# Weight groups prepared one cell later, and a halo requested ahead of the first weights

## The chip, the cores and the metric

The kernel runs on one core of a Trainium2 chip. A core has five engines that each work through their own list of instructions in order: PE multiplies matrices, DVE and POOL work on vectors, ACT copies, casts and evaluates functions, and SP here only issues transfers, which 16 DMA engines carry out. The metric is device time in microseconds (us) of one execution; lower is better.

## The reference

A causal convolution over time with weights that differ per token and head, and after it two feed-forward layers. Shapes: x is (2, 4096, 192), there are 8 heads of 24 channels and 7 taps, and the layers go from 192 to 2048 and back to 192, for all 8192 tokens.

```python
# convolution: softmax over the 7 taps, then a weighted sum of 7 tokens
w = weight_gen - np.max(weight_gen, axis=-1, keepdims=True)
w = np.exp(w)
w = w / (np.sum(w, axis=-1, keepdims=True) + 1e-09)
x_pad = np.concatenate([np.zeros((B, 6, D)), x], axis=1)
x_unf = x_pad[:, np.arange(S)[:, None] + np.arange(K)[None, :], :].reshape(B, S, K, H, group)
x = np.einsum('bshk,bskhg->bshg', w, x_unf).reshape(B * S, D)
# first layer
h = x @ moe_w_in
g = np.where(h > 0.0, h, np.exp(np.minimum(h, 0.0)) - 1.0)
x = g @ moe_w_out
# second layer
h = x @ moe2_w_in
g = h * np.clip(h + 3.0, 0.0, 6.0) / 6.0
out = g @ moe2_w_out
```

x and weight_gen are float32. The layers' weight matrices are float64 in memory, which is why the kernel reads them as pairs of 32-bit words.

## The kernel before, in words

**Tiling.** The 128 partitions each own 64 tokens in a row. The tokens are taken in 16 *blocks* of 4 tokens per partition (512 tokens). Each layer's 2048 hidden columns are taken in 8 *slices* of 256. A *cell* is one layer, one block, one slice: 2 x 16 x 8 = 256 cells, first all of the first layer, then all of the second (`cells`, lines 494 and 495). Cell n is number n in that list, and cells 0 to 7 are block 0 of the first layer.

**Precision.** Products are made of two parts: x is split into xh and xl, a weight into a high part (`wi_h`, in `wo` the first columns) and a low part (`wi_l`), and three of the four cross products are summed. A cell has 18 matmuls for the first product (x by w_in into the two PSUM tiles `h`), and from cell 3 on the second product of the cell three before (g by w_out into `acca` and `accb`; `LAG` is 3).

**What a cell does outside PE.** ACT evaluates the activation from `h` (line 468 and 469, twice each, one per half), DVE ends it (line 485, `gate`), ACT rounds the result to the high part gh (line 475, `round_g`), DVE makes the low part gl (line 479, `rest_g`). A cell's `h` tiles are used again two cells on, so the gate has to be done by then.

**Weights.** They don't come ready: the 64-bit words have to be turned into a high and a low part on the core. A *unit* is one slice of w_in (kind i) or w_out (kind o). `groups` (line 544) puts the first layer's units together: group 0 is the first slice of w_in, groups 1 to 7 are two units each, group 8 is one. A unit of the first layer takes one step on ACT (`begin`, line 146), five on DVE (lines 150, 153, 157, 165, 174; at 157 ACT also casts the high part, line 167), then three matmuls on PE (`p5`, lines 179 to 181: their sum is the low part), and ACT's casts of that sum (`p6`, line 186). In groups 1 to 3 the intermediate words lie in the PSUM bank that `p5` writes next, so that `p5` has to wait for the last DVE step; from group 4 on they lie in SBUF.

**What orders it.** All of it is written out by hand in the loop at line 604; nothing is reordered after that. In cell n come: the matmuls of cell n; `p5` of group n+1; `round_g` of cell n-1 (while n is 1 to 7); activation and gate of both halves, with `p6` of group n+1 after them; then `wst.run(n)`, which issues the ACT and DVE steps of later groups; then `rest_g`. How many steps `run` issues follows from a table of tasks: each has a cell from which it may begin, a *due* cell and a count of steps, and enough steps are issued to have each task done before its due cell. For a unit group n of the first layer the due cell stands in line 545. When a group begins, the transfers of the next group's raw words are requested (`want`).

**Before cell 0** (lines 582 to 602) two things are made side by side: the convolution of block 0, half of it on DVE and half on POOL, and group 0. DVE's list takes their steps in turns. `load_block` (line 204) requests a block's tap weights `wt`, its own tokens in `xt`, and for blocks 0 and 1 the *halo*, the tokens before the block that another partition owns, by two transfers of 63 rows (line 218). For block 0 `between` is the request of group 0's raw words: three transfers. SP issues these requests one after the other in the order of the list.

Of the kernel before, what the change touches and what calls it, by code (L numbers as in the profile page):

```python
# [17 lines left out]
def kernel(  # L18
# [185 lines left out]
    def load_block(i, between=None):  # L204
        t0 = TM * i
        xt = xw.tile([P, TM + HALO, D], F32, tag="xt", name="xt", bufs=2)
        wt = xw.tile([P, TM * H, K], F32, tag="wt", name="wt", bufs=2)
        later(
            0, wt.rearrange("p a k -> p (a k)"), wv[:, t0:t0 + TM, :].rearrange("p t c -> p (t c)"))
        m = max(0, HALO - t0)  # L210
        later(0, xt[:, m:HALO + TM, :], xv[:, t0 - HALO + m:t0 + TM, :])
        if between:
            between()
        if m:

            for b in range(B):
                nc.gpsimd.memset(xt[b * PB:b * PB + 1, 0:m, :], 0.0)
                nc.sync.dma_start(
                    xt[b * PB + 1:(b + 1) * PB, 0:m, :],
                    xv[b * PB:(b + 1) * PB - 1, TP + t0 - HALO:TP + t0 - HALO + m, :])  # L220
        return xt, wt

    def attention(i):
# [283 lines left out]
    def later(n, out, in_):  # L507

        if now is None or now >= len(cells) or now < 2 and n == 0:
            nc.sync.dma_start(out, in_)  # L510
        else:
            waiting.append((now + n, out, in_))
# [29 lines left out]

    units = [(k, 0, q - (k == "o")) for q in range(NQ + 1) for k in "io" if 0 <= q - (k == "o") < NQ]
    groups = [units[:1]] + [units[n:n + 2] for n in range(1, len(units), 2)]
    wtasks = [[0, n - 2, len(g)] for n, g in enumerate(groups)]
    for n in range(2 * NQ):
        c = NQ * (n + 2) if n < NB - 2 else start2 + (NQ if n % 2 else 0)
        groups.append([("io"[n % 2], 1, n // 2)])
# [9 lines left out]
    def w_steps(n):  # L558
        def step(k, u):
            def s():  # L560
                if k < 0:
                    if u == 0:
                        want(n)
                        want(n + 1)
                        if groups[n][0][1] == 0:

                            fts[n] = act.tile([P, XN], F32, tag="z", name="f", bufs=2)
                    made[n][u].begin()
                else:
                    getattr(made[n][u], f"s{k}")()  # L570
            return s
        return [step(k, u) for k in range(-1, WS if groups[n][0][1] else 5) for u in range(len(groups[n]))]

    wtasks = [
        [b, d, ((WS if groups[n][0][1] else 5) + 1) * c, (lambda n: lambda: w_steps(n))(n)] for n, (b, d, c) in enumerate(wtasks) if n > 1]
# [5 lines left out]
    with tc.manual_schedule():  # L581
        nc.vector.memset(three, 3.0)
        nc.scalar.activation(warm, three, AF.Exp)
        blk[0] = load_block(0, lambda: want(0))
        make_identity(nc, ident)
        nc.scalar.copy(plus, ident)
        nc.scalar.mul(minus, ident, -1.0)
        blk[1] = load_block(1)

        todo = {"w": w_steps(0), "a": attention(0)}  # L590
# [13 lines left out]
        for n in range(len(cells) + LAG + 3):  # L604
# [54 lines left out]
            if n in loads:  # L659
                blk[loads[n]] = load_block(loads[n])  # L660
# [30 lines left out]
```

## Time and profile before

| | before |
|---|---|
| runs outside the profiler | 1232.46, 1232.89, 1233.21 us; median 1232.89 |
| span of the profiled execution | 1230.4 us |
| PE busy | 1193.3 us (97%) |
| weight loads of PE | 1053.3 us (86%) |
| DVE busy | 933.1 us (76%) |
| ACT busy | 855.9 us (70%) |
| POOL busy | 418.7 us (34%) |
| moved by DMA | 75.81 MB |

The span runs from the first to the last instruction. What lies between it and a run's time (2.49 us to the median) is start and end outside the instructions; the profile gives no other time of its own. PE is busy for all but 37 us. Where an engine sat idle ahead of an instruction, the trace names what released it.

### The profile page before, as it was taken

How to read it: one execution, taken by the hardware profiler on the slowest of the kernel's cores; microseconds unless marked ns; L12 is line 12 of the kernel's file. 1: busy time of each engine (PE TensorE's matmuls, PEld its weight loads, DVE VectorE, ACT ScalarE, POOL GpSimd, SP SyncE). 2: the span in 40 equal slices, each digit the busy share in tenths (PEclk: the TensorE clock that was granted, in tenths of full speed). 3: DMA queues.
4: the chain of work that ended last, by engine and by line, in shares of the span. 5: the costliest groups of instructions: out<-in, count | busy, mean ns of one | idle time of the engine just before them, and what ended most of it. 6: DMA issues, size and time to landing. Idle time of an engine off the chain costs nothing.

```text
span 1230.4 us, 25449 instructions
## 1 busy us (share of the span) xinstructions
PE 1193.3 (97%) x10176; PEld 1053.3 (86%) x10176; DVE 933.1 (76%) x1224; ACT 855.9 (70%) x1340; POOL 418.7 (34%) x234
## 2 busy tenths in 40 slices
PE   3799999999999999999999999999999999999998
PEld 2568898989999888999888888888888888888886
DVE  6778999999999999998677666666666666666663
ACT  2677888888888888888876665555666665666653
POOL 7438778877777877776000000000000000000000
PEclk9899999999999999999999999999999999999999
DMA  6432023222122222111211101111110111111110
GB/s 175 125 114 65 25 88 88 88 88 69 41 69 87 89 88 77 67 39 47 65 53 52 41 31 48 52 52 40 52 38 29 52 52 52 40 52 33 34 40 26
DMA packets 33430, 75.81 MB, mean 62 GB/s; under 512 B 4388, under 2 KB 16802, under 8 KB 33312
## 3 DMA queue, kind: packets, MB, share of 16 engines
q1 hardware_dynamic: 33312, 74.19, 20.8%
q8 instruction: 80, 1.31, 0.5%
q14 instruction: 38, 0.31, 0.1%
HBM read 36.43 MB, written 12.58 MB: 40 GB/s over the span
## 4 chain that ended last, share of the span: by engine, by line
PE 92%; DVE 3%; ACT 3%; DMA 1%; issue 1%; SPq 0%; DVEq 0%
PE h L448 43%; PE acca L448 29%; PE accb L448 19%; DVE gl L479 1%; ACT gh L475 1%; DMA xt<-in_x_dram 1%; DVE r L485 0%; ACT r L468 0%; ACT r L469 0%; PE acca L316 0%; DVE f L157 0%; PE acca L372 0%; PE acca L179 0%; PE aux L179 0%; DMA xl<-xl 0%
## 5 line engine op out<-in xcount | busy, mean ns | idle before, releaser
L448 PE MATMUL h<-xh,wi_l 64*128 64x512 f32 x1536 | 577.7, 397 | 4.8 <-ACT wi_l L186 4.8
L448 PE MATMUL h<-xh,wi_h 64*128 64x512 f32 x1536 | 572.7, 396 | 3.2 <-DVE xl L328 2.6
L448 PE MATMUL h<-xl,wi_h 64*128 64x512 f32 x1536 | 570.2, 395 | 0.8 <-DMA xl<-xl 0.8
L448 PE MATMUL acca<-gh,wo 64*128 64x512 f32 x2048 | 561.9, 393 | 0.3
L479 DVE TENSOR_TENSOR gl<-r,gh 128x1024 fp32r<-128x1024 f32 x256 | 394.6, 1541 | 63.3 <-ACT gh L475 62.1
L448 PEld LDWEIGHTS acca<-gh,wo 64*128 64x128 f32 x2048 | 378.0, 185 | 27.3 <-SPq L452 2.4
L471 ACT ACTIVATE r<-h,three 128x512 f32<-128x512 f32 x256 | 176.2, 688 | 222.7 <-PE h L448 114.9
L448 PE MATMUL accb<-gh,wo 64*128 64x512 f32 x1024 | 324.7, 396 | 0.0
L448 PE MATMUL accb<-gl,wo 64*128 64x512 f32 x1024 | 321.3, 393 | 0.3 <-DVE gl L479 0.3
L448 PE MATMUL acca<-gl,wo 64*128 64x512 f32 x1024 | 321.2, 393 | 0.0
L448 PEld LDWEIGHTS h<-xh,wi_l 64*128 64x128 f32 x1536 | 284.9, 186 | 24.6 <-ACT wi_l L186 6.0
L448 PEld LDWEIGHTS h<-xh,wi_h 64*128 64x128 f32 x1536 | 284.9, 186 | 23.0 <-DVE xl L328 2.8
L448 PEld LDWEIGHTS h<-xl,wi_h 64*128 64x128 f32 x1536 | 284.3, 186 | 20.1 <-DMA xl<-xl 1.4
L488 DVE SCALAR_TENSOR_TENSOR r<-r,h 128x512 f32<-128x512 f32 x256 | 175.9, 687 | 161.2 <-ACT r L471 160.4
L475 ACT CAST gh<-r 128x1024 fp32r<-128x1024 f32 x256 | 266.3, 1040 | 11.2 <-DVE r L485 10.5
L485 DVE SCALAR_TENSOR_TENSOR r<-r,h 128x512 f32<-128x512 f32 x256 | 173.2, 677 | 40.3 <-ACT r L469 39.5
L448 PEld LDWEIGHTS acca<-gl,wo 64*128 64x128 f32 x1024 | 189.4, 185 | 12.5
L448 PEld LDWEIGHTS accb<-gl,wo 64*128 64x128 f32 x1024 | 189.0, 185 | 12.7 <-DVE gl L479 0.7
L448 PEld LDWEIGHTS accb<-gh,wo 64*128 64x128 f32 x1024 | 186.6, 185 | 12.0 <-issue 1.4
L274 POOL TENSOR_TENSOR tmp<-xt,wt 128x768 f32<-128x768 f32 (+1 forms) x96 | 192.6, 2006 | 6.3
L468 ACT ACTIVATE r<-h 128x512 f32<-128x512 f32 x256 | 152.5, 596 | 51.8 <-PE acca L448 30.3
L469 ACT ACTIVATE r<-r 128x512 f32<-128x512 f32 x256 | 162.0, 633 | 8.1
(119 smaller groups left out, 731.1 us busy)
## 6 DMA issues: line engine op xcount, KB each, us to landing
xt<-in_x_dram SPq DMA_DIRECT2D x14, 960.0 KB, 5.5
xh<-xh SPq DMA_DIRECT2D x64, 192.0 KB, 2.7
xl<-xl SPq DMA_DIRECT2D x64, 192.0 KB, 2.8
raw<-in_moe_w_out_dram SPq DMA_DIRECT2D x16, 384.0 KB, 3.2
z<-z SPq DMA_DIRECT2D x16, 384.0 KB, 2.3
zin<-z SPq DMA_DIRECT2D x16, 384.0 KB, 3.0
out_dram<-ot SPq DMA_DIRECT2D x16, 384.0 KB, 4.0
raw<-in_moe_w_in_dram SPq DMA_DIRECT2D x16, 192.0 KB, 3.3
```

What stands on the lines that cost most here:

```text
L274: eng.tensor_tensor(o.rearrange("p t (h g) -> p t h g", g=G), xk, wk.rearrange("p (t h) g -> p t h g", h=H), op=ALU.mult)
L448: mm = nc.tensor.matmul(o, w, r, start=st, stop=sp).ins
L468: nc.scalar.activation(r, h, AF.Relu, scale=-1.0)
L469: nc.scalar.activation(r, r, AF.Exp, scale=-1.0)
L471: nc.scalar.activation(r, h, AF.Relu, bias=three)
L475: nc.scalar.copy(gg[n][0], rs[n])
L479: nc.vector.tensor_tensor(gl, rs.pop(n), gh.bitcast(F32), op=ALU.subtract)
L485: nc.vector.scalar_tensor_tensor(r, r, -1.0, h, op0=ALU.add, op1=ALU.max)
L488: nc.vector.scalar_tensor_tensor(r, r, 6.0, h, op0=ALU.min, op1=ALU.mult)
```

## The change

Two edits. In `load_block` the callback `between` is called behind the halo's requests where there is a halo, and ahead as before where there is none; only block 0 passes one. In the table of tasks the due cell of weight group n of the first layer goes from n-2 to n-1.

```diff
@@ load_block
         later(0, xt[:, m:HALO + TM, :], xv[:, t0 - HALO + m:t0 + TM, :])
-        if between:
+        if between and not m:
             between()
         if m:
 
             for b in range(B):
                 nc.gpsimd.memset(xt[b * PB:b * PB + 1, 0:m, :], 0.0)
                 nc.sync.dma_start(
                     xt[b * PB + 1:(b + 1) * PB, 0:m, :],
                     xv[b * PB:(b + 1) * PB - 1, TP + t0 - HALO:TP + t0 - HALO + m, :])
+            if between:
+                between()
         return xt, wt
@@ tasks of the weight groups
-    wtasks = [[0, n - 2, len(g)] for n, g in enumerate(groups)]
+    wtasks = [[0, n - 1, len(g)] for n, g in enumerate(groups)]
```

The first edit shows on SP, at the start of the program. `wt` and `xt` are block 0's tap weights and tokens, `63x1152` its halo, `raw` the words of weight group 0, and the last row is block 1's tap weights. Before:

```order
L510 DMA wt<-in_weight_gen_dram 128x224
L510 DMA xt<-in_x_dram 128x768
L510 DMA raw<-in_moe_w_in_dram 64x3x256
L510 DMA raw<-in_moe_w_in_dram 64x2x256
L510 DMA raw<-in_moe_w_in_dram 64x256
L218 DMA xt<-in_x_dram 63x1152 x2
L510 DMA wt<-in_weight_gen_dram 128x224
```

With the change:

```order
L512 DMA wt<-in_weight_gen_dram 128x224
L512 DMA xt<-in_x_dram 128x768
L218 DMA xt<-in_x_dram 63x1152 x2
L512 DMA raw<-in_moe_w_in_dram 64x3x256
L512 DMA raw<-in_moe_w_in_dram 64x2x256
L512 DMA raw<-in_moe_w_in_dram 64x256
L512 DMA wt<-in_weight_gen_dram 128x224
```

The two halo requests have moved past the three of the weights; DVE's, ACT's and POOL's lists at this place are as before, with group 0's steps at the same places between those of the convolution.

The second edit shows on ACT between cells 0 and 1. The first two rows are the casts of group 2's high parts, `gh` is the rounding of cell 0, `h_75` and `h_74` are cell 1's halves, `wi_l<-accb` is the low part of group 2, and `aux<-raw` with `acca_77<-raw` begin group 3. Before:

```order
L167 CAST wi_h<-f 128x384
L167 CAST wo_88<-f 128x2x192
L146 ACTIVATE aux<-raw 128x384
L146 ACTIVATE acca_77<-raw 128x384
L167 CAST wi_h<-f 128x384
L167 CAST wo_88<-f 128x2x192
L475 CAST gh<-r 128x1024
L468 ACTIVATE r<-h_75 128x512
L469 ACTIVATE r<-r 128x512
L468 ACTIVATE r<-h_74 128x512
L469 ACTIVATE r<-r 128x512
L186 CAST wi_l<-accb 128x384
```

With the change:

```order
L167 CAST wi_h<-f 128x384
L167 CAST wo_88<-f 128x2x192
L477 CAST gh<-r 128x1024
L470 ACTIVATE r<-h_75 128x512
L471 ACTIVATE r<-r 128x512
L470 ACTIVATE r<-h_74 128x512
L471 ACTIVATE r<-r 128x512
L186 CAST wi_l<-accb 128x384
L186 CAST wo_88<-acca_76 128x2x128
L186 CAST wo_88<-acca_76 128x2x64
L146 ACTIVATE aux<-raw 128x384
L146 ACTIVATE acca_77<-raw 128x384
```

Group 3's steps have moved from cell 0 to behind the activations of cell 1 and the low part of group 2. On DVE its ten steps move likewise behind cell 1's two gates, and groups 4 to 8 each move one cell on, so that group 8's steps come in cell 6, where there were none. PE's list holds the same instructions in the same order. SP requests the raw words of groups 4 to 8 one cell later, and the loads of block 2 and of the second layer's first weights change places with some of them.

## Rows read from the trace of the kernel before

**Rows 1.** Waits of PE, 22 to 76.5 us: who waited for whom, total, times, longest.

```profile
PE h L448 <- ACT wi_l L186: 4.8, 2, 4.5
...
PE accb L179 <- DVE boot L174: 2.3, 1, 2.3
PE acca L316 <- ACT wo L186: 1.5, 1, 1.5
```

**Rows 2.** Busy time by stretch: span of it, engines, granted clock, DMA share, GB/s.

```profile
29.40:31.60 2.20, 2.20 (x9) 1.40 (x8) 1.23 (x2) 1.63 (x3) 2.12 (x2) 1.00 0.86 237
31.60:34.80 3.20, 3.19 (x19) 2.44 (x18) 2.07 (x5) 1.41 (x4) 3.04 (x3) 1.00 0.10 36
39.97:44.46 4.49, 0.01 (x2) 0.01 (x1) 3.20 (x7) 4.43 (x9) 4.33 (x4) 0.82 0.93 300
44.46:53.10 8.64, 8.64 (x24) 6.16 (x24) 6.47 (x14) 5.93 (x12) 0.04 (x1) 0.50 0.46 116
53.27:57.90 4.63, 4.63 (x39) 3.54 (x38) 3.43 (x10) 3.10 (x7) 0.00 (x0) 1.00 0.30 82
```

**Rows 3.** Timeline of ACT, 32 to 59 us: start, duration, instruction, idle before it.

```profile
32.16 0.54 ACT L146 ACTIVATE accb<-raw 128x384 f32<-128x384 f32 x1
...
35.18 0.51 ACT L167 CAST wi_h<-f 128x384 fp32r<-128x384 f32 x1 [2.04 <-DVE f L157]
35.64 0.51 ACT L167 CAST wo<-f 128x384 fp32r<-128x384 f32 x1
...
40.69 1.04 ACT L475 CAST gh<-r 128x1024 fp32r<-128x1024 f32 x1
41.64 0.59 ACT L468 ACTIVATE r<-h 128x512 f32<-128x512 f32 x1
...
43.94 0.46 ACT L186 CAST wi_l<-accb 128x384 fp32r<-128x384 f32 x1
...
44.72 1.03 ACT L146 ACTIVATE f<-raw 128x384 f32<-128x384 f32 x2
...
49.02 0.59 ACT L468 ACTIVATE r<-h 128x512 f32<-128x512 f32 x1
...
58.06 0.59 ACT L468 ACTIVATE r<-h 128x512 f32<-128x512 f32 x1
```

**Rows 4.** Timeline of PE at 37 us.

```profile
37.05 0.59 PE L179 MATMUL accb<-f,ident 128*128 128x384 f32 x1 [2.26 <-DVE boot L174]
```

**Rows 5.** Timeline of all engines, 0 to 20 us.

```profile
1.67 2.04 SPq L510 DMA_DIRECT2D raw<-in_moe_w_in_dram  x3
...
3.75 0.89 SPq L218 DMA_DIRECT2D xt<-in_x_dram  x2
...
4.67 0.36 SPq L510 DMA_DIRECT2D wt<-in_weight_gen_dram  x1
...
6.59 0.51 ACT L146 ACTIVATE aux<-raw 128x384 f32<-128x384 f32 x1 [2.25 <-DMA raw<-in_moe_w_in_dram]
...
7.13 0.57 DVE L150 TENSOR_SCALAR aux<-aux 128x384 f32<-128x384 f32 x1 [1.28 <-ACT aux L146]
...
8.07 0.56 DVE L153 TENSOR_SCALAR aux<-aux 128x384 uint32<-128x384 uint32 x1
...
10.84 0.56 DVE L274 TENSOR_TENSOR h<-xt,h 128x384 f32<-128x384 f32 x1 [2.21 <-DMA xt<-in_x_dram]
...
18.60 0.46 POOL L292 TENSOR_TENSOR y<-y,tmp 128x128 f32<-128x128 f32 x1
...
19.03 0.69 PE L316 MATMUL h<-ident,y 64*128 64x64 f32 x8 [2.92 <-DVE y L292]
```

**Rows 6.** The chain that ended last, at the start: start, duration, what.

```profile
4.35 6.37 DMA xt<-in_x_dram
```

**Rows 7.** Transfer issued at 4.67 us: count, KB, us from issue to landing.

```profile
wt<-in_weight_gen_dram SPq DMA_DIRECT2D x1, 112.0 KB, 6.2
```

**Rows 8.** Busy time by stretch, as rows 2, while the halo was under way.

```profile
4.30:10.72 6.42, 0.00 (x0) 0.00 (x0) 2.88 (x8) 0.55 (x2) 4.43 (x6) 1.00 0.88 233
```

## The prediction, made before the change was run

> **What bounds the kernel now.** First the page's busy times: PE is busy for 1193.3 of 1230.4 us, so only PE's 37 us of idleness and the time at a lower clock can be won. Then the waits of PE: nearly all of that idleness lies ahead of 76.5 us. Behind that PE is hardly idle, so a change in the first cells moves all that follows by the same amount. Behind the start, the waits to look at are 4.5 us for ACT's cast of a low weight part (`wi_l`), 2.3 us for DVE's last step of a group (`boot`), and 1.5 us for ACT's `wo` [rows 1]. Third, the table by stretch: the 4.49 us are the stretch from 39.97 us, in which the granted clock falls, and the next 8.64 us run at 0.50 of the full clock, 1.2 instead of 2.4 GHz [rows 2]. So the wait is paid twice. Fourth, ACT's timeline: between group 2's casts at 35.18 and 35.64 and cell 0's rounding at 40.69 it only serves group 3 and waits for DVE in it; cell 1's activation comes at 41.64, and the cast that PE waits for at 43.94 [rows 3]. Last, the first 20 us, where the convolution of block 0 waits 2.21 us on DVE for the halo [rows 5].
>
> **The due cells.** *What goes.* Group 3's steps leave the place between group 2 and cell 1. ACT is then free behind the second cast of group 2, at 35.64 + 0.46 (the distance of the two casts) = 36.10. The rounding takes 0.95 (40.69 to 41.64), so cell 1's activation starts at 37.05 instead of 41.64, and `wi_l` comes 2.30 behind it (41.64 to 43.94), at 39.35, done at 39.8 [rows 3]. PE needs it at 39.97. The 4.49 us go, and with them the reason that the clock fell.
>
> *What is late next.* Group 3 now begins behind group 2's casts: 0.78 behind `wi_l` (43.94 to 44.72), at 40.13 [rows 3]. Its `p5` has to wait for DVE's last step, as group 2's did: there ACT began at 32.16 and PE was released at 37.05, 4.89 later [rows 3, 4]. So PE is released at 45.0. It gets there at 37.05 + 2.2 (a group's `p5` at full clock) + 3.2 (a cell) = 42.4 [rows 2, 4]: a new wait of 2.6 us. With `p5` cell 3 starts at 45.0 + 2.2 = 47.2; before it started at 53.27 [rows 2]. That is 6.1 us earlier.
>
> *What is given back.* ACT's round for a cell with a full group is 7.38 us (41.64 to 49.02); PE's is 4.63 + 2.20 = 6.83 [rows 2, 3]. So ACT sets the pace until the groups run out, before and with the change. Group 3's round is longer, since its words lie in PSUM: from its start to its cast 3.02 (32.16 to 35.18) instead of 2.46 (44.72 to 47.18) [rows 3]. With it cell 2's activation starts at 40.13 + 3.02 + 0.46 + 0.46 + 0.95 = 45.0 and cell 3's at 45.0 + 7.38 = 52.4, against 58.06 [rows 3]: 5.7 us are left. Before, cell 5 had only the one unit of group 8 and cell 6 none; now cell 5 has two, cell 6 one. The second unit in cell 5 costs ACT one more start and one more cast, 0.46 each, 0.9 us, of which PE's slack at that place hides some 0.2; in cell 6 the group fits beside PE. So 5.0 us arrive. From both sides: 6.1 if nothing is given back; 3.3 if the clock falls in the new wait (below). A loss is excluded: the same steps are issued, and each group still ahead of its `p5`.
>
> The requests that move with it have room: the words of groups 5 to 8 are asked for in the cell ahead of the one that uses them, as before.
>
> **The halo's place.** *What it wins.* SP spends 0.89 us on the two halo requests and 2.04 on the three of the weights; the halo is asked for at 1.67 instead of 3.75 [rows 5]. It landed at 10.72, 4.35 + 6.37 [rows 6], and DVE's product for the second tap, the first that reads it, began at 10.84 [rows 5]. If that were all, DVE would win up to 1.4 us.
>
> *What it costs.* DVE's list takes turns: group 0's first step (line 150) stands ahead of the first tap's product, and line 153 ahead of the second's. Line 150 waits for ACT at 6.59, which waits for the weights [rows 5]. If they come later, DVE stands still however early the halo is. Between ACT's start and the second tap's product lie 0.54 (6.59 to 7.13), 0.94 (two instructions, 7.13 to 8.07) and 0.47 for line 153: 1.95 us [rows 5].
>
> When do the weights land behind the halo? The nearest row is the 112 KB asked for right behind it at 4.67, which took 6.2 us and so landed at 10.9, just after the halo [rows 7]. In the new order the weights stand there, with the same bytes ahead of them as the halo had; I take 10.7. Then ACT starts at 10.8, the second tap's product at 12.75, 1.9 us later than before. The bounds: a gain of 1.3 if the weights don't feel the halo at all, a loss of 2.5 if they land as late as 11.3.
>
> By the Trainium skill (DMA: Bandwidth & Descriptors, "Queues, rings and completion order") each DMA engine takes up its descriptors in the order of its ring; rows 7 agree, and by that rule alone the loss is the same 1.9. By the same page ("Why a DMA increments its semaphore by 16 and not by 1") a transfer is spread over the largest number up to 16 that divides its outer size: 63 rows would lie on 9 engines, 63 KB on each, an estimate that no row here shows and that would keep the weights on those nine waiting.
>
> *What hides it.* Nothing on DVE, which works without a pause from there to the last tap. POOL's half ends at 18.60 + 0.46 = 19.06, and PE's transposes wait for DVE until 19.03 [rows 5]. The two halves end together, so a later DVE moves block 0's first matmul by the whole amount, and an earlier one would gain only where DVE's own work behind it (block 1's softmax) is in the way. The later start moves all of the first cells, as each waits in turn for ACT and DVE: +1.9.
>
> **Sum.** -5.0 + 1.9 = -3.1 us: the span 1230.4 becomes 1227.3. The median of the runs lies 2.5 above the span, which neither edit touches: 1232.9 becomes **1229.8**.
>
> **Rivals.**
> - *The halo costs the weights only its share of the bandwidth.* While the halo was under way the core moved 233 GB/s [rows 8]; 567 KB are 2.4 us of that. The weights, there at 6.5 before (ACT starts at 6.59) [rows 5], would land at 8.9, the second tap's product would begin at 11.0, a loss of 0.2. Against it: the small transfer of rows 7, which waited longer. Time: 1232.9 - 4.8 = 1228.1.
> - *The halo was the bound.* The weights are fetched beside it and DVE gains 1.3: 1226.6. Against it: rows 7 again.
> - *The clock falls in the new wait.* In the wait of 4.49 us it was down to 0.50 for the last 1.6 us (0.82 on average), so it fell after some 2.9 us; in the 2.26 us ahead of 37.05 it was not lost [rows 2, 4]. The new wait of 2.6 lies between. If it falls, cell 3's activation comes 9.04 behind cell 2's, as before (49.02 to 58.06), not 7.38 [rows 3]: 1.7 us. Time: 1231.5.
> - *Slower: the clock falls a second time.* The groups of cells 4 to 7 now come just in time. If ACT is late there too and one of these waits reaches some 2.9 us, PE runs another 8.64 us at 0.50 in which it does what takes 3.2 + 2.2 at full clock, 3.2 us lost [rows 2], on top of the rival before: -1.4 + 3.2, 1234.7. Against it: by the rounds above these waits are 0.5 us each. It decides only if ACT's round is over 2 us longer than the 7.38 of the rows.
>
> **How the numbers follow.** The forecast gets 0.49, its own range 1228.6 to 1231.2 (the weights between 9.7 and 11.3, and 0.8 either way for the point at which the clock rises in cell 0). The share of bandwidth 0.16, the halo as the bound 0.07, the clock in the new wait 0.23, the second fall 0.05. The range 1227.2 to 1232.4 leaves out the second fall, most of the case with the halo as the bound, and the tails. A difference under 0.2%, 2.5 us, can't be told from none: faster means below 1230.4. That is 0.7 of the forecast, nearly all of the two cases below it and a little of the clock case, 0.59; slower by 0.2% is over 1235.4, 0.04 with the tails; the rest, 0.37, is within.
>
> **What the profile of the changed kernel would show.** Right: the wait on `wi_l` of 4.5 us is gone; a wait of 2 to 3 us ahead of group 3's `p5`, on `boot`; no stretch at clock 0.50 after the start; cell 3 some 4 us earlier than 53.27. At the start ACT's first `raw` step near 10.8, DVE's second tap's product near 12.7 with no wait of its own for the halo, and PE's first transposes near 21. Wrong: ACT's first step ahead of 9 us (a rival of the start is true), a stretch at 0.50 behind 45 us (the clock), or PE waits of over 1 us ahead of `p5` in cells 4 to 7 (the pace of ACT's rounds is mis-sized).

## The result, and the profile of the changed kernel

| | before | changed |
|---|---|---|
| median of the runs | 1233.05 us (4 runs) | 1240.03 us (1238.91 to 1241.6, 4 runs) |
| ratio, 95% interval | 1 | 1.0057 (1.0042 to 1.0071) |
| span of the profiled execution | 1230.4 us | 1237.1 us |

The change makes the kernel 7.0 us slower, where 3.1 us faster was forecast and 1232.4 was the range's end. The profiled execution of the changed kernel is the shortest of its four runs (1238.91 us), so the two spans differ by 6.7 us.

**Part of the forecast is there.** PE's waits in the changed kernel, 20 to 125 us, total, times, longest, to be held against [rows 1]:

```profile
PE h L450 <- DVE xl L330: 2.6, 1, 2.6
PE acca L181 <- DVE boot L174: 2.6, 1, 2.6
PE aux L179 <- DVE boot L174: 2.4, 1, 2.4
PE accb L179 <- DVE boot L174: 2.3, 1, 2.3
...
PE acca L179 <- DVE f L157: 1.4, 1, 1.4
...
PE h L450 <- ACT wi_l L186: 0.3, 1, 0.3
```

The wait of 4.5 us on `wi_l` is gone (the 0.3 in the last row is another one, at 83.09 us), and a wait of 2.4 us on group 3's `boot` (`aux`) has come, as forecast. New and not forecast are the waits of 1.4 us on line 157 and 2.6 us on `boot` for `acca`: both belong to group 8. ACT's timeline, which answers to [rows 3]:

```profile
38.95 0.51 ACT L167 CAST wo<-f 128x384 fp32r<-128x384 f32 x1
39.37 1.04 ACT L477 CAST gh<-r 128x1024 fp32r<-128x1024 f32 x1
40.32 0.59 ACT L470 ACTIVATE r<-h 128x512 f32<-128x512 f32 x1
...
42.62 0.46 ACT L186 CAST wi_l<-accb 128x384 fp32r<-128x384 f32 x1
```

Cell 1's activation comes at 40.32 and the low part of group 2 at 42.62. The distance is 2.30, as before; only the round of group 3 is gone from in front of them.

**The start is later than forecast.** The first 26 us, all engines, to be held against [rows 5]:

```profile
1.67 0.72 SPq L218 DMA_DIRECT2D xt<-in_x_dram  x2
...
2.43 2.04 SPq L512 DMA_DIRECT2D raw<-in_moe_w_in_dram  x3
...
4.51 0.59 SPq L512 DMA_DIRECT2D wt<-in_weight_gen_dram  x1
...
12.21 0.52 ACT L146 ACTIVATE aux<-raw 128x384 f32<-128x384 f32 x1 [7.87 <-DMA raw<-in_moe_w_in_dram]
...
12.75 0.57 DVE L150 TENSOR_SCALAR aux<-aux 128x384 f32<-128x384 f32 x1 [6.90 <-ACT aux L146]
...
14.16 0.55 DVE L276 TENSOR_TENSOR h<-xt,h 128x384 f32<-128x384 f32 x1
...
25.86 0.79 PE L450 MATMUL h<-xh,wi_h 64*128 64x512 f32 x1 [2.62 <-DVE xl L330]
```

Block 0's first matmul before:

```profile
22.55 0.79 PE L448 MATMUL h<-xh,wi_h 64*128 64x512 f32 x1 [2.61 <-DVE xl L328]
```

The transfer behind the weights with the change, which answers to [rows 7]:

```profile
wt<-in_weight_gen_dram SPq DMA_DIRECT2D x1, 112.0 KB, 7.8
```

The weights landed at 12.1 (ACT starts at 12.21), not at 10.7. DVE's second tap's product starts at 14.16 instead of 10.84, without a wait of its own, and block 0's first matmul at 25.86 instead of 22.55. Both are 3.3 us later.

**Where the loss is.** PE's transposes of block 1 divide the first cells from what follows. After, and then before:

```profile
74.66 0.25 PE L318 MATMUL acca<-ident,y 64*128 64x64 f32 x1 [1.49 <-ACT wo L186]
```

```profile
76.46 0.25 PE L316 MATMUL acca<-ident,y 64*128 64x64 f32 x1 [1.48 <-ACT wo L186]
```

Here the changed kernel is still 1.8 us *ahead*: +3.3 from the start, -5.1 from the groups. What follows is group 8 in cell 6, with DVE, POOL and PE in three fences (start, duration, instruction, idle before it):

```profile
83.96 1.31 DVE L150 TENSOR_SCALAR f<-f 128x384 f32<-128x384 f32 x1 [0.56 <-ACT f L146]
85.30 1.89 DVE L153 TENSOR_SCALAR f<-f 128x384 uint32<-128x384 uint32 x1
87.23 1.78 DVE L157 SCALAR_TENSOR_TENSOR f<-raw,f 128x384 uint32<-128x384 uint32 x1
89.04 1.86 DVE L165 TENSOR_SCALAR tr<-f 128x384 uint32<-128x384 uint32 x1
90.94 1.78 DVE L174 SCALAR_TENSOR_TENSOR boot<-raw,tr 128x384 fp32r<-128x384 uint32 x1
92.65 2.84 DVE L481 TENSOR_TENSOR gl<-r,gh 128x1024 fp32r<-128x1024 f32 x1
```

```profile
83.51 1.54 POOL L276 TENSOR_TENSOR tmp<-xt,wt 128x768 f32<-128x768 f32 x1
85.13 1.85 POOL L283 TENSOR_TENSOR y<-y,tmp 128x768 f32<-128x768 f32 x1
87.05 1.54 POOL L276 TENSOR_TENSOR tmp<-xt,wt 128x768 f32<-128x768 f32 x1
88.67 2.01 POOL L283 TENSOR_TENSOR y<-y,tmp 128x768 f32<-128x768 f32 x1
90.76 1.54 POOL L276 TENSOR_TENSOR tmp<-xt,wt 128x768 f32<-128x768 f32 x1
```

```profile
89.16 0.88 PE L179 MATMUL acca<-f,ident 128*128 128x384 f32 x2 [1.35 <-DVE f L157]
...
92.78 0.69 PE L181 MATMUL acca<-boot,plus 128*128 128x384 f32 x1 [2.57 <-DVE boot L174]
```

Before, the same five steps of DVE stood in cell 5, ahead of POOL's start at 82.50:

```profile
78.51 0.35 DVE L150 TENSOR_SCALAR f<-f 128x384 f32<-128x384 f32 x1
78.90 0.36 DVE L153 TENSOR_SCALAR f<-f 128x384 uint32<-128x384 uint32 x1
79.30 0.56 DVE L157 SCALAR_TENSOR_TENSOR f<-raw,f 128x384 uint32<-128x384 uint32 x1
...
80.28 0.56 DVE L174 SCALAR_TENSOR_TENSOR boot<-raw,tr 128x384 fp32r<-128x384 uint32 x1
80.76 1.22 DVE L479 TENSOR_TENSOR gl<-r,gh 128x1024 fp32r<-128x1024 f32 x1
...
82.50 1.54 POOL L274 TENSOR_TENSOR y<-xt,wt 128x768 f32<-128x768 f32 x1 [38.00 <-DMA xl<-xl]
...
84.29 2.34 DVE L479 TENSOR_TENSOR gl<-r,gh 128x1024 fp32r<-128x1024 f32 x1
```

The five steps took 0.35 to 0.56 us each; now they take 1.31 to 1.89. Each ends some 0.2 to 0.4 us behind the end of one of POOL's instructions (85.05, 86.98, 88.59, 90.68, 92.30 are start plus duration of POOL's rows): DVE gets one step done for each of POOL's. The two rows of line 479 show that the trace of before had this already: the low part gl takes 1.22 us with POOL idle and 2.34 beside it.

PE waits 1.35 + 2.57 us for these steps; the last matmul of `p5` ends at 92.78 + 0.69 = 93.47, where before it ended at 89.70 + 0.34 = 90.04:

```profile
89.70 0.34 PE L181 MATMUL acca<-boot,plus 128*128 128x384 f32 x1
```

From 1.8 ahead it has come to 3.4 behind. In cell 8 PE then waits for a low part that DVE also made beside POOL (the row of 92.65 above, 2.84 us):

```profile
95.54 0.79 PE L450 MATMUL accb<-gl,wo 64*128 64x512 f32 x1 [0.92 <-DVE gl L481]
```

By stretch (stretch, its length, busy us of PE, its loads, DVE, ACT and POOL, clock, DMA share, GB/s), which answers to the row of 0.50 in [rows 2]:

```profile
49.60:53.00 3.40, 3.40 (x12) 2.15 (x12) 2.07 (x5) 2.83 (x7) 0.00 (x0) 0.50 0.01 2
82.00:88.00 6.00, 5.54 (x40) 3.86 (x40) 5.05 (x5) 1.89 (x6) 5.84 (x4) 1.00 0.59 196
...
90.00:93.90 3.90, 1.33 (x5) 0.79 (x5) 3.87 (x3) 3.14 (x7) 3.74 (x3) 0.57 0.00 1
93.99:100.60 6.61, 5.69 (x28) 4.03 (x26) 4.96 (x6) 2.21 (x4) 6.37 (x4) 0.50 0.01 2
```

From 82 to 88 us PE is busy but for 0.5 us and the clock is 1.00; in the second wait it falls (0.57 on average from 90.0 to 93.9), and it is at 0.50 up to 100.6 us. Cell 9 begins at 101.98, before at 94.51: the loss is 7.5 us there. Some 0.8 of it comes back at 134 us, where PE waits once more in the kernel before (0.60 us on DVE's line 485) and not in the changed one. So the profile adds up: +3.31 (start) - 5.11 (groups up to cell 6) + 5.23 (group 8) + 4.03 (cell 8: 0.92 of waiting for gl, the rest at 1.2 GHz) - 0.77 (the wait at 134 us) = +6.69, the difference of the spans.

### The profile page after: what moved, and what is told of

Same layout as the page of the kernel before. It is cut to its first block, busy times and chain, and to the rows that moved or that the text cites. A ratio compares the mean times of both kernels' runs of the same rounds, so it can differ in the third digit from the quotient of the medians.

```text
span 1237.1 us, 25443 instructions
## 1 busy us (share of the span) xinstructions
PE 1194.4 (97%) x10176; PEld 1067.3 (86%) x10176; DVE 936.9 (76%) x1224; ACT 855.6 (69%) x1340; POOL 416.5 (34%) x234
## 3 DMA queue, kind: packets, MB, share of 16 engines
q8 instruction: 80, 1.31, 0.5%
## 4 chain that ended last, share of the span: by engine, by line
PE 91%; DVE 4%; ACT 2%; DMA 1%; issue 1%; SPq 0%; DVEq 0%; ACTq 0%
PE h L450 42%; PE acca L450 28%; PE accb L450 19%; DVE gl L481 1%; DMA raw<-in_moe_w_in_dram 1%; ACT gh L477 0%; DVE f L157 0%; DMA xl<-xl 0%; PE acca L318 0%; ACT r L471 0%; ACT r L470 0%; DVE r L487 0%; DVE h L276 0%; DMA raw<-in_moe_w_out_dram 0%; PE aux L374 0%
## 5 line engine op out<-in xcount | busy, mean ns | idle before, releaser
L450 PEld LDWEIGHTS accb<-gh,wo 64*128 64x128 f32 x1024 | 187.5, 186 | 10.9 <-issue 1.5
```

The source lines that it names most:

```text
L450: mm = nc.tensor.matmul(o, w, r, start=st, stop=sp).ins
```

## The experiments

All times are medians of runs beside runs of the kernel before (median 1233.09 us in both sets of runs); the 95% interval is that of the ratio to it. The changed kernel's 1240.03 stood beside 1233.05.

### Each edit alone

The first edit alone (the due cell stays n-2):

```diff
-    wtasks = [[0, n - 1, len(g)] for n, g in enumerate(groups)]
+    wtasks = [[0, n - 2, len(g)] for n, g in enumerate(groups)]
```

> Before, with the first edit alone (block 0's halo requested ahead of group 0's words). Theory: the weights wait behind the halo as in the changed kernel, the first matmul of block 0 comes 3.3 us later (25.86 instead of 22.55 us) and nothing behind it hides that: 1233 + 3.3 = about 1236.3. Rival: the late start only costs because the groups come due late; with the groups as before it is taken up by the wait of 4.5 us on the low part, and the time is 1233 to 1234.

Measured: 1236.05 us, ratio 1.0020 (1.0011 to 1.0029), 3.0 us slower. The theory holds, the rival is out. In its profiled execution (1234.15 us) the first matmul came at 24.30, only 1.75 later; the landing of the weights differs between executions (ACT's first step at 10.64 here, 12.21 above).

The second edit alone:

```diff
-    wtasks = [[0, n - 2, len(g)] for n, g in enumerate(groups)]
+    wtasks = [[0, n - 1, len(g)] for n, g in enumerate(groups)]
```

> Before, with the second edit alone (weight groups of the first layer due one cell later). Theory: cell 6 begins 5 us earlier than before (71.4 instead of 76.5), then group 8's five steps on DVE run beside POOL's convolution of block 2 at 1.3 to 1.9 us each, PE waits for them and loses its clock, which costs 8 to 9 us; net 3 to 4 us slower, about 1236.7. Rival: the collision is only there because the halo's edit moved the start; then the gain stays and the time is 1228.

Measured: 1237.63 us, ratio 1.0030 (1.0019 to 1.0040), 4.5 us slower. The collision doesn't need the other edit. The two losses add up to 7.5, and both edits together cost 7.0. Cell 6 was later than expected: PE's transposes came at 73.78, 50.6 us behind the first matmul instead of 48.8. The clock went another way in this execution. It rose later: `p5` of group 1 still ran at the lower level (1.10 us for line 180 at 31.08, 0.63 in the changed kernel), so that cell 1 began 11.1 us behind cell 0 and not 9.1. And it fell in cell 2 already (0.50 from 41.05 to 47.80).

### The collision taken away, in two ways

The second edit, and group 8's words in a PSUM bank:

```diff
-                if self.n > 3:
+                if 3 < self.n < 8:
                     self.b = self.f
...
-            if self.m == 0 and self.n < 4:
+            if self.m == 0 and not 3 < self.n < 8:
                 self.r = self.b
```

> The second edit alone, and group 8's intermediate words in a PSUM bank (as groups 1 to 3 have them) instead of SBUF. Theory: DVE's steps on words in PSUM are not held up beside POOL (groups 1 to 3 took 0.55 us a step beside POOL's block 1), so the five steps take 0.5 to 0.6 us each, PE doesn't wait ahead of cell 8, and the gain of the first cells stays: 1228, 5 us faster than before. Rival: the steps are slow because of the transfers under way at that time (DMA share 0.5 to 0.9), or for any reason that has nothing to do with where the words lie; then they take over 1.3 us again and the time is as with the second edit alone.

Measured: 1229.64 us, ratio 0.9967 (0.9955 to 0.9979), 3.5 us faster than before. DVE's timeline in that kernel; POOL works on block 2 from 79.31:

```profile
81.37 0.57 DVE L150 TENSOR_SCALAR acca<-acca 128x384 f32<-128x384 f32 x1 [0.66 <-ACT acca L146]
...
82.57 0.56 DVE L157 SCALAR_TENSOR_TENSOR f<-raw,acca 128x384 uint32<-128x384 uint32 x1
...
83.76 0.55 DVE L174 SCALAR_TENSOR_TENSOR boot<-raw,acca 128x384 fp32r<-128x384 uint32 x1
```

The same steps, at the same place beside the same POOL, take 0.55 to 0.57 us, though POOL is busy for 2.84 of the 3 us from 82 to 85, and the DMA engines for 0.93 of their time (columns as above):

```profile
82.00:85.00 3.00, 3.00 (x25) 2.23 (x21) 2.90 (x5) 1.84 (x3) 2.84 (x3) 1.00 0.93 299
```

So it is where the words lie, and not the transfers; in the changed kernel, too, line 174 took 1.78 us in a stretch with a DMA share of 0.00 (90.0 to 93.9). The gain is 3.5 us, and the 5 that were expected lie inside its interval (2.6 to 5.5). In this execution the groups bring 5.1 up to the transposes, as above (71.97, 48.8 behind the first matmul; before, 53.9). The start is 0.6 later (first matmul at 23.17), and 1.1 is given back behind the transposes (0.7 was forecast, for cells 5 and 6), so that 3.4 are left in the span (1227.0 us). The clock fell for a while here, too, at the end of group 3's `p5` and in cell 3 (0.50 from 46.95 to 50.30).

Both edits, with POOL leaving out five of block 2's seven taps:

```diff
-        for k in range(K - 2, -1, -1):
+        for k in range(K - 2, -1, -1) if i != 2 else [0]:
```

> The changed kernel, group 8's words in SBUF as there, but POOL leaves out five of the seven taps of block 2 (taps 2 to 6 of seven in the order in which they are added; the values of block 2 are not the reference's). Theory: DVE's five steps of group 8 are held up only while POOL works: the ones that fall beside POOL's few remaining instructions (some 6 us from 82 us) still take over 1.3 us, those behind them 0.36 to 0.56; the time falls by 3 to 6 us against the changed kernel. Rival: the steps are slow for another reason; all five take 1.3 to 1.9 us as before, and the time stays at 1240.

Measured: 1231.44 us, 8.6 below the changed kernel. DVE and POOL there:

```profile
85.05 1.31 DVE L150 TENSOR_SCALAR f<-f 128x384 f32<-128x384 f32 x1 [0.57 <-ACT f L146]
86.39 1.34 DVE L153 TENSOR_SCALAR f<-f 128x384 uint32<-128x384 uint32 x1
87.77 0.97 DVE L157 SCALAR_TENSOR_TENSOR f<-raw,f 128x384 uint32<-128x384 uint32 x1
88.77 0.36 DVE L165 TENSOR_SCALAR tr<-f 128x384 uint32<-128x384 uint32 x1
89.17 0.56 DVE L174 SCALAR_TENSOR_TENSOR boot<-raw,tr 128x384 fp32r<-128x384 uint32 x1
```

```profile
86.22 1.29 POOL L287 TENSOR_TENSOR y<-y,tmp 128x512 f32<-128x512 f32 x1
87.48 0.85 POOL L297 TENSOR_TENSOR y<-y,tmp 128x256 f32<-128x256 f32 x1
```

POOL ends at 87.48 + 0.85 = 88.33. Up to there DVE's steps are stretched, behind it the same kind of step takes 0.36 and 0.56. It is POOL that holds DVE up. The expected gain was too small, since it left out what followed the wait in the changed kernel, the 4.0 us of cell 8; here the clock is 1.00 there (90 to 101 us).

### Both edits without the collision

The changed kernel with group 8's words in PSUM, the same two lines as above:

> The changed kernel (both edits) with group 8's words in PSUM. Theory: what made the changed kernel slow beyond the halo's cost was the collision of group 8's steps with POOL; without it the two edits come out as the sum of the halo alone (+3.0) and the groups (-3.5): 1232.6, within 0.2% of before. Rival: the late start brings a loss of its own with the later groups (more waits ahead of their matmuls, another fall of the clock); then 1235 or more.

Measured: 1232.45 us, ratio 0.9990 (0.9981 to 0.9999). The theory holds: the edits come out as the sum of their parts, and the 7.6 us between this kernel and the changed one (1240.03 - 1232.45) hang on where group 8's words lie.

### The halo

In the old order, each halo request split:

```diff
-                nc.sync.dma_start(
-                    xt[b * PB + 1:(b + 1) * PB, 0:m, :],
-                    xv[b * PB:(b + 1) * PB - 1, TP + t0 - HALO:TP + t0 - HALO + m, :])
+                for r0, r1 in ((0, 48), (48, PB - 1)):
+                    nc.sync.dma_start(
+                        xt[b * PB + 1 + r0:b * PB + 1 + r1, 0:m, :],
+                        xv[b * PB + r0:b * PB + r1, TP + t0 - HALO:TP + t0 - HALO + m, :])
```

> Before, with each halo request of 63 rows split into one of 48 and one of 15 rows, in the old order. Theory A: a transfer of 63 rows uses only some of the DMA engines, so the split one lands clearly earlier than 10.7 us; DVE's second tap's product starts at 9 to 10 instead of 10.84 and the time falls by up to 1.3 us, to about 1232. Theory B: the bytes set the landing, not the number of rows; the halo lands at 10.7 or a little later for the two additional requests, and the time is 1233 to 1234.

Measured: 1231.81 us, ratio 0.9986 (0.9977 to 0.9995), 1.3 us faster. DVE's second tap's product there:

```profile
9.88 0.56 DVE L275 TENSOR_TENSOR h<-xt,h 128x384 f32<-128x384 f32 x1 [1.11 <-DMA xt<-in_x_dram]
```

It starts at 9.88, though SP issues four requests instead of two; in the last version below, with the same requests, it starts at 9.72. In three executions with 63-row requests in the same order it started at 10.84, 11.45 and 11.49. That speaks for theory A; which engines carried which rows, no row shows. Block 0's first matmul came at 21.74, 0.8 us earlier than before and not 1.0: POOL's half of the convolution now ends last (18.59 + 0.60 = 19.19, while PE's transposes of DVE's half begin at 18.07). So an earlier DVE wins only up to POOL's end.

The halo first and split (the first edit and the same split):

> The first edit alone, with the halo's requests split into 48 and 15 rows. Theory: the weights land late behind the halo because 63 rows load only some of the DMA engines; spread over more of them the halo passes faster and the weights land at 9 instead of 10.6 to 12.1 us; DVE's second tap's product starts near 11, and the time is 1233 to 1234 instead of 1236. Rival: the weights wait for the halo's bytes whatever the spread; 1236.

Measured: 1234.63 us, ratio 1.0006 (0.9997 to 1.0015). The landing that the theory named didn't come: ACT's first step stands at 10.60, as in the first edit alone (10.64), and DVE's second tap's product at 12.55. But SP issued the weights' first request 1.1 us later here (3.49 instead of 2.41, behind four requests instead of two), and it took 5.9 us to land, where it took 7.0 to 8.7 us in the four executions with the unsplit halo ahead. So in this one execution the weights passed faster, and the two more requests took that back. The medians are 1.4 us apart and the two intervals just overlap: what the split is worth in this order is not settled. In no execution with the halo ahead did the weights land by 9.

### A version that beats both

The second edit, group 8's words in PSUM, the old order with the split halo:

> The second edit, group 8's words in PSUM, the halo in its old place and its requests split into 48 and 15 rows. Theory: the gains of the two parts add, since the split moves the start and the groups move what follows: 1229.6 - 1.3 = about 1228.4. Rival: the earlier start is taken up by ACT's rounds or by a fall of the clock in the first cells; then 1229.6 or a little above.

Measured: 1228.85 us, ratio 0.9961 (0.9947 to 0.9974), 4.2 us faster than before and 11 faster than the change. That is 0.8 below the version without the split. The expected 1228.4 and the rival's 1229.6 both lie in the interval (1226.6 to 1229.9), so that these runs can't tell whether the gains add in full.

## Why the prediction was wrong

- **The wait on `wi_l` and what is late next: right.** Cell 2's wait of 4.5 us is gone, the new one ahead of group 3 was 2.4 for a forecast 2.6, and up to the transposes of block 1 the groups brought 5.1 us (forecast 5.7 at that place). The clock fell at the end of group 3's `p5` and was at 0.50 for 3.4 us (49.60 to 53.00 in the table above): the rival, at a smaller price than the 1.7 that it was given. ACT waited 0.32 us for that `p5`, and its rounds of cells 2 and 3 took 7.8 and 7.9 us, where the first was forecast at 7.38 and the second took 7.66 before: this is the missing 0.6.
- **The step that failed** is in the part on what is given back: "in cell 6 the group fits beside PE". It sized group 8's steps by the durations that the other groups' steps had. Those ran with POOL idle (groups 4 to 8 before) or on words in PSUM (groups 1 to 3). In cell 6 POOL works on block 2, and five steps that took 2.3 us from first to last took 8.8 (83.96 to 92.72). That put 5.2 us in PE's way where the sum had nothing, and cell 8 another 4.0 behind it. The experiments with PSUM and with POOL's taps left out show it from both sides.
- **"A loss is excluded"** fell with it. The argument counted steps and their order against `p5`, and not what runs on POOL at their new place. Of the rivals, the slower one had a late group and a fallen clock, which is what happened at group 8; but DVE beside POOL made the group late, and not a long round of ACT, which that rival asked for. So its sign, waits of over 1 us ahead of `p5`, came (1.35 and 2.57) for another reason.
- **The halo's loss was set too low:** 1.9 forecast, 3.0 measured (edit alone; its interval, 1.4 to 3.6, still holds the 1.9), 3.3 in the profile. The order of the mechanism was right (DVE stands behind line 150, which stands behind the weights). With the unsplit halo ahead ACT's first step came at 10.64, 11.49, 11.99 and 12.21 in four executions, and block 0's first matmul 1.75, 2.6, 3.1 and 3.3 us later than before; 11.3 was too tight a bound for the landing. The step that set it took the same bytes ahead to mean the same landing, and these four have the same requests in the same order. The 112 KB behind the weights took 6.2, 7.2, 7.6 and 7.8 us there. The profile of before, from which the loss was counted, has its halo's reader 0.6 earlier than two other executions of that order (10.84 against 11.45 and 11.49).
- **Both rivals that let the halo's edit cost next to nothing or gain are out**, by the edit alone.
- **The 2.5 us between span and median** are not all start and end outside the instructions. A run's own span is 1.8 us shorter than its time (1238.91 and 1237.1 in the changed kernel); the rest is that the profiled execution of before was shorter than its median. That changed nothing in the forecast's difference.

## What to carry to other kernels

When a step moves, look up what the *other* engines do at its new place, and take its duration from rows in which they do the same; for steps on SBUF, a mean over a stage in which POOL was idle is worth nothing for one in which it works. A place with slack and a place on the way to PE differ by more than the wait: here 5.2 us of lateness took another 3.1 with the clock. And a request moved to the front of a queue is paid by the one that it passes: find out which of the two is first in the list of the engine that waits.

## What the runs showed of the hardware

- **DVE on SBUF beside POOL.** A step of 128 x 384 words in SBUF took 0.35 to 0.56 us alone and 1.31 to 1.89 beside POOL; the same steps with their words in PSUM took 0.54 to 0.57 beside it, and line 174 at 48.15 in the changed kernel, with POOL idle since 47.84, took 0.55 as well. The Trainium skill has this (SBUF — State Buffer, "Who interferes with whom"): DVE and GpSimd (POOL here) share one pair of SBUF ports under an exclusive lock, which a DVE instruction needs when it has two SBUF inputs or runs in a two-port mode, and whoever comes second waits for the other's whole instruction. The rows above agree: DVE's steps end one for one 0.2 to 0.4 us behind POOL's. It works both ways: POOL's product at 94.47 in the changed kernel, issued while DVE's gl ran to 95.49, took 2.41 us instead of 1.54.
- **The clock's fall is not at one place.** With the second edit it fell behind waits of 2.2 to 2.5 us ahead of `p5`, of group 2 in two executions (the second edit alone, and POOL's taps left out) and of group 3 in four, though the instructions of PE, ACT and DVE up to there are the same. In those two the clock had risen later in the first cells, too: cell 1 began 11.1 and 10.9 us behind cell 0, in the changed kernel 9.1. What decides that was not tried.
- **A transfer's landing at the start differs between executions** of the same requests: the halo's reader started at 10.84 to 11.49 us in the old order, the weights' at 10.64 to 12.21 with the unsplit halo ahead.
